# Second expert layer: pairs of token tiles under stationary weights, then single tiles

## The chip, the cores and the metric

One core of a Trainium2 chip runs the whole program. The metric is the device time of one execution in microseconds (us), lower is better. The engines that matter are TensorE (PE in the profile, with its weight loads shown apart as PEld), VectorE (DVE), ScalarE (ACT), GpSimd (POOL) and SyncE (SP), which here only starts transfers. A matmul holds one 128x128 operand still in the array (the stationary operand, brought in by a weight load) and streams the other past it (the moving operand, up to 512 columns).

## The reference

Attention with pooled keys and values makes 4608 tokens of width 512; a dense layer follows, then a routed layer of 8 experts, each token going to one expert:

```python
x = attention(q, k, v)                   # (4608, 512)
h = x @ moe_w_in                         # first layer, width 2048
x = maximum(0.01 * h, h) @ moe_w_out
logits = x @ moe2_w_gate                 # second layer, 8 experts
expert_idx = argmax(logits, axis=1)
for e in range(8):
    m = expert_idx == e
    h = maximum(x[m] @ w1[e], 0)         # w1[e]: 512 x 1024
    out[m] = gate_w[m] * (h @ w2[e])     # w2[e]: 1024 x 512
```

With the reference's inputs the experts get 1165, 549, 12, 0, 597, 0, 571 and 1714 tokens. In tiles of 128 tokens that is 10, 5, 1, 0, 5, 0, 5 and 14, in all 40 tiles.

## The kernel before

Every float32 product is made from two halves, a high part and the rest (index 0 and 1 of an operand), in three passes: high by high, high by rest, rest by high.

*First layer.* The tokens go through in 18 blocks of 256, each in 16 slots, one for each 128 columns of the hidden width. `g1` (L488) multiplies stationary weights with the block's 256 columns in 12 matmuls of 256; ACT and DVE make the activation and its two halves (`ghl`, two buffers); `g2` (L514) uses those halves as stationary operand and streams the weights, 6 matmuls of 512, into the two PSUM banks y0 and y1. `g2` runs two slots behind `g1`. At the end of a block `y_evac` (L529) copies both banks out on ACT. A table of hooks places the attention of later blocks, the splitting of the experts' weights, the logits and the routing in these slots. `step_consts` (L731, in slot 36) prepares constants for the later list of steps.

*Early list.* In the last block, whose slots are counted from k0, `early_1` (slot k0+7) picks the expert with most tokens so far and fetches the list of its first four tiles; `early_2` (slot k0+10) transposes that list on PE (`unpack`, L642) and issues the gathers of its first three tiles. `w_load` brings that expert's weights in four pieces of 2 MB, in slots 9, 10, 11 and 15.

*Second layer.* A step is one tile of 128 tokens of one expert. The token rows are gathered by GpSimd (`m_gather`, L814). `m_xT` (L824) transposes them on PE in four 128x128 transposes, and ACT and DVE write the two halves. `m_g1` (L835) takes the tokens as stationary operand and streams the weights: 2 times 12 matmuls of 512 columns. The hidden rows come out with tokens on the partitions, so `m_hT` (L848) transposes them back on PE, 2 times four transposes, and ACT and DVE write their halves. `m_g2` (L858) does 2 times 12 matmuls of 512; ACT scales the result by the gate (L873) and GpSimd scatters the rows out (L874).

There are two sets of weight tiles (lanes). Steps 0 to 3 use lane 0; later steps alternate. Lane 0 walks the list of tiles from its start, lane 1 from its end. When a lane's expert changes, its next weights are loaded piece by piece behind a condition (`w_next`, L801). The list of the 36 later tiles is made in `final` (L672) and `final_list` (L718), on DVE, once all tokens are routed, while the first two tiles are worked on. Steps 0 to 39 always run, the last three only where the list is that long (L1182).

Of the kernel before, what the change touches and what calls it, by code (L numbers as in the profile page):

```python
# [11 lines left out]
I32 = mybir.dt.int32  # L12
# [9 lines left out]
def kernel(  # L22
# [33 lines left out]
    NX = NSTEP - 3  # L56
    PB = NB - TPB
# [566 lines left out]
    stepc = pool.tile([P, 4], F32, name="stepc")  # L624
# [28 lines left out]
    def early():  # L653
        V = nc.vector
        c = count(0)
        tmp = sb([P, 1, E], F32, "etmp")
        first_max(c, ohs, mb, tmp, 1)
        V.tensor_scalar(out=es, in0=mb, scalar1=-1.0, scalar2=float(E), op0=ALU.mult, op1=ALU.add)
        rows = sb([P, 1], F32, "erow")
        V.scalar_tensor_tensor(  # L660
            out=rows, in0=mb, scalar=-float(CAP), in1=prow, op0=ALU.mult, op1=ALU.add
        )
        ri = sb([P, 1], I32, "eri")
        V.tensor_copy(ri, rows)
        V.tensor_copy(itab[:, NR, 0:1], es)
        V.memset(etab[:, 0:1], -1.0)
        V.tensor_copy(etab[:, 1:2], es)
        V.tensor_scalar(out=rank0, in0=ohs[:, 0], scalar1=4096.0, scalar2=None, op0=ALU.mult)
        V.tensor_tensor(out=rank0, in0=rank0, in1=rev8, op=ALU.add)
        return fetch(ri[0:NE, 0:1], NE, 0)  # L670

    def final(c):  # L672
# [10 lines left out]
        m = sb(sq, F32, "g", 2)  # L683
        key = sb([P, E], F32, "fk")
        V.scalar_tensor_tensor(out=key, in0=n, scalar=float(E), in1=rank0, op0=ALU.mult, op1=ALU.add)
        pre = sb([P, E], F32, "fp")
        end = sb([P, E], F32, "fe")
        ft = sb([P, 4], F32, "ft")
        tot, T, row = ft[:, 0:1], ft[:, 1:2], ft[:, 2:3]
        cv = sb([P, 2], F32, "fcv")  # L690
        V.tensor_reduce(tot, n, axis=AX.X, op=ALU.add)
        V.tensor_tensor(out=m, in0=bc(key, sq, 1), in1=bc(key, sq, 2), op=ALU.is_gt)
        V.tensor_copy(itab[0:1, NR, 1:2], tot[0:1])
        V.tensor_tensor(out=m, in0=m, in1=bc(n, sq, 1), op=ALU.mult)
        V.tensor_reduce(pre, m, axis=AX.X, op=ALU.add)
        V.scalar_tensor_tensor(out=T, in0=stepc[:, 0:1], scalar=tot, in1=stepc[:, 1:2], op0=ALU.mult, op1=ALU.add)
        V.tensor_tensor(out=cv[:, 1:2], in0=stepc[:, 2:3], in1=tot, op=ALU.is_lt)
        V.tensor_tensor(out=end, in0=pre, in1=n, op=ALU.add)
# [5 lines left out]
        V.scalar_tensor_tensor(out=base, in0=iota8, scalar=float(CAP), in1=pre, op0=ALU.mult, op1=ALU.subtract)  # L704
        V.tensor_tensor(out=sel, in0=sel, in1=s2, op=ALU.mult)
        V.scalar_tensor_tensor(out=base, in0=ohs[:, 0], scalar=float(NE), in1=base, op0=ALU.mult, op1=ALU.add)
        V.tensor_tensor(out=s2, in0=sel, in1=iota8, op=ALU.mult)
        V.tensor_tensor(out=base, in0=sel, in1=base, op=ALU.mult)
        V.tensor_reduce(cv[:, 0:1], s2, axis=AX.X, op=ALU.add)
        V.tensor_reduce(row, base, axis=AX.X, op=ALU.add)  # L710
        V.tensor_scalar(
            out=T, in0=T, scalar1=float(E * CAP), scalar2=cv[:, 1:2], op0=ALU.subtract, op1=ALU.mult
        )
        ri = sb([P, 1], I32, "fri")
        V.scalar_tensor_tensor(out=ri, in0=row, scalar=float(E * CAP), in1=T, op0=ALU.add, op1=ALU.add)
        return ri, cv

    def final_list(cv):  # L718
        V = nc.vector
        p = pt("att")  # L720
        for j in range(2):
            nc.tensor.matmul(
                p[0:1, j * 64:j * 64 + NR], cv[0:NR, j:j + 1], ident[0:NR, 0:NR], start=True, stop=True
            )
        er, ch = etab[0:1], sb([1, NR], F32, "fch")
        V.tensor_copy(er[:, 2:], p[0:1, 0:NR])
        V.tensor_copy(itab[0:1, 0:NR, 0], p[0:1, 0:NR])
        V.tensor_tensor(out=ch, in0=er[:, 2:], in1=er[:, 0:NR], op=ALU.not_equal)
        V.tensor_tensor(out=itab[0:1, 0:NR, 1], in0=ch, in1=p[0:1, 64:64 + NR], op=ALU.mult)

    def step_consts():  # L731
        V = nc.vector
        pi = sb([P, 2], I32, "spi")
        pf = sb([P, 2], F32, "spf")
        t, od = pf[:, 0:1], pf[:, 1:2]
        nc.gpsimd.iota(pi[:, 0:1], pattern=[[0, 1]], base=0, channel_multiplier=1)
        V.tensor_copy(stepc[:, 2:3], pi[:, 0:1])
        V.tensor_scalar(out=pi[:, 1:2], in0=pi[:, 0:1], scalar1=1, scalar2=None, op0=ALU.bitwise_and)
        V.tensor_scalar(out=pi[:, 0:1], in0=pi[:, 0:1], scalar1=1, scalar2=None, op0=ALU.arith_shift_right)
# [39 lines left out]
    def hT_view(t, j):  # L779
        return hT_a[:, j] if t % 2 == 0 else vm[j]  # L780

    def lane(t):
        return 0 if t < NE or (t - NE) % 2 else 1
# [12 lines left out]
    def w_regs(s):  # L796
        e = nc.sync.value_load(itab[0:1, s, 0:1], min_val=0, max_val=E - 1)
        c = nc.sync.value_load(itab[0:1, s, 1:2], min_val=0, max_val=1) if s < NR else None
        regs[s] = (e, c)

    def w_next(t, pieces):  # L801
        s2 = t + 2 - NE
        if t < NE - 1 or s2 >= NR:
            return
        if t == NE - 1:
            s2 = 1
        if pieces[0] == 0:
            w_regs(s2)
        e, c = regs[s2]
        w_load(lane(t), pieces, e, c)  # L810
# [3 lines left out]
    def m_gather(t):  # L814
        x = sb([P, DM], F32, "ps", 3)
        n = PB * BLK if t < NE else NT
        nc.gpsimd.indirect_dma_start(
            out=x, out_offset=None, in_=y_d[0:n],
            in_offset=bass.IndirectOffsetOnAxis(ap=gidx[:, t:t + 1], axis=0), bounds_check=n - 1,
            oob_is_err=False,  # L820
        )
        xg[t] = x

    def m_xT(t):  # L824
# [6 lines left out]
        sub(nc.vector, xT2[:, t % 2, :, 1], pv, f32(xT2[:, t % 2, :, 0]))  # L831

# [25 lines left out]
    def m_g2(t, j):  # L858
# [12 lines left out]
        if j == 1:  # L871
            o = sb([P, DM], F32, "kv", 2)
            nc.scalar.activation(o, o_ps.pop(t), AF.Copy, scale=gate[:, t:t + 1])  # L873
            nc.gpsimd.indirect_dma_start(  # L874
                out=out, out_offset=bass.IndirectOffsetOnAxis(ap=sidx[:, t:t + 1], axis=0), in_=o,
                in_offset=None, bounds_check=NT - 1, oob_is_err=False,
            )
# [87 lines left out]
    def early_2():  # L965
        unpack(early_list.pop(0), NE, 0)
        for t in range(3):
            m_gather(t)
# [20 lines left out]
    with tc.manual_schedule():  # L989
# [93 lines left out]
        for s, (b, f) in enumerate(seq):  # L1083
# [31 lines left out]
            if s == k0 + 10:  # L1115
                early_2()
# [3 lines left out]
        m_xT(0)  # L1120
        m_gather(3)
# [5 lines left out]
        m_g1(0, 0)  # L1127
        y_tr(b, 0)
        y_tr(b, 1)
        m_g1(0, 1)  # L1130
        y_logit(b)
        m_hT(0, 0)
        route_a(b)
        m_xT(1)
        m_g2(0, 0)
        m_hT(0, 1)
        route_b(b)
        route_c(b, 0)
        route_c(b, 1)
        m_g2(0, 1)  # L1140
        cnt = count(1)
        m_g1(1, 0)
        ri, cv = final(cnt)
        m_g1(1, 1)
        final_list(cv)
        m_hT(1, 0)
        m_xT(2)
        w_regs(0)
        early_list[0] = fetch(ri[0:NR, 0:1], NR, NE)
        w_load(1, [0, 1], *regs[0])  # L1150
        m_hT(1, 1)

        def steps(t0, t1):
            for t in range(t0, t1):
                m_g1(t, 0)
                if t > t0 or t == 2:
                    m_g2(t - 1, 0)
                m_g1(t, 1)
                w_next(t, [0, 1])
# [3 lines left out]
                if t == 2:  # L1163
                    unpack(early_list.pop(0), NR, NE)
                    m_gather(4)
                    nc.sync.value_load(gidx[0:1, NE:NE + 1], min_val=0, max_val=NT - 1)
                    w_load(1, [2, 3], *regs[0])
                if t > t0 or t == 2:
                    m_g2(t - 1, 1)
                    if t - 1 >= NE - 1:  # L1170
                        w_next(t - 1, [2, 3])
# [5 lines left out]
            if t1 < NSTEP:  # L1177
                w_next(t1 - 1, [2, 3])

        steps(2, NX)  # L1180
# [40 lines left out]
```

## Time and profile before

| | |
|---|---|
| median of 3 runs | 1572.53 us (1563.01 to 1573.03) |
| profiled execution | 1560.74 us |
| its span, first to last instruction | 1559.0 us |
| granted TensorE clock, mean | 0.985 |
| PE busy | 1482.3 us, 95% of the span |
| DVE, ACT, POOL busy | 920.3, 643.8, 327.6 us |

The time of a run is that of the device; the span leaves out what lies before the first and after the last instruction, here 1.7 us. The profiled execution is faster than the fastest of the three others. Busy shares are means over stages that have different limits, so the stretches are read one by one.

### The profile page before, as it was taken

Reading aid. Unit: us, or ns where it says so; the run is one execution under the profiler, and the core shown is the slowest. Engines: PE = TensorE matmul, PEld = TensorE weight load, DVE = VectorE, ACT = ScalarE, POOL = GpSimd, SP = SyncE. Lnnn points to the kernel's source line nnn. Section 1 sums busy time; section 2 is a strip of 40 time slices with the busy share of each in tenths; the row PEclk is TensorE's granted clock in tenths of the full one; section 3 lists DMA queues with packets and bytes.
Section 4 is the critical chain, followed back from the end, with each engine's and each line's share of the span. In section 5 each row is a group of like instructions: output and inputs, shape, how many; then the busy total and the mean of one; then the engine's idle time right before and its main releaser. Section 6 shows DMA issues by size and latency. Waiting matters only on the chain. (4 is left out here: it accounts for less than half of the span.)

```text
span 1559.0 us, 25084 instructions
## 1 busy us (share of the span) xinstructions
PE 1482.3 (95%) x8824; PEld 1296.9 (83%) x8824; DVE 920.3 (59%) x2371; ACT 643.8 (41%) x1442; POOL 327.6 (21%) x294
## 2 busy tenths in 40 slices
PE   4598999999999999999999999999999999999998
PEld 3476889899898898899999899977888888888886
DVE  6998768878878878877878887743111111111111
ACT  4676534544544454544444444322222222222222
POOL 4000012223232222222232233021111111111111
PEclk8799999999999999999999999999999999999999
DMA  9543135456445555545655454064721331661250
GB/s 213 148 134 100 73 127 166 158 198 186 159 150 195 171 183 159 186 154 178 176 167 189 140 181 153 17 238 168 299 84 41 149 147 41 248 264 47 67 231 22
DMA packets 121384, 238.01 MB, mean 153 GB/s; under 512 B 56845, under 2 KB 65041, under 8 KB 117544
## 3 DMA queue, kind: packets, MB, share of 16 engines
q1 hardware_dynamic: 90312, 139.81, 29.0%
q10 hardware_dynamic: 23328, 76.56, 12.9%
q0 software_dynamic: 7616, 20.01, 3.9%
q8 instruction: 71, 1.16, 0.3%
q14 instruction: 57, 0.47, 0.1%
HBM read 418.44 MB, written 87.38 MB: 324 GB/s over the span
## 5 line engine op out<-in xcount | busy, mean ns | idle before, releaser
L522 PE MATMUL y<-w,ghl 128*128 128x512 f32 x1728 | 461.2, 403 | 3.8 <-DVE ghl L128 3.7
L522 PEld LDWEIGHTS y<-w,ghl 128*128 128x128 f32 x1728 | 306.1, 189 | 62.0 <-DVE ghl L128 7.8
L128 POOL TENSOR_TENSOR ps<-ps 128x512 f32<-128x512 f32 x128 | 182.5, 1426 | 477.2 <-ACT ps L125 366.7
L494 PEld LDWEIGHTS h<-x_t,w 128*128 128x128 f32 x1776 | 238.2, 194 | 39.8 <-DVE w L128 18.2
L494 PE MATMUL h<-x_t,w 128*128 128x256 f32 x1776 | 245.7, 288 | 24.0 <-DVE w L128 16.8
L494 PEld LDWEIGHTS y<-x_t,w 128*128 128x128 f32 x1488 | 193.2, 189 | 9.7
L542 DVE CUSTOM_DVE_ANT_0 junk<-y,wg 128x512 bf16<-128x512 f32 x256 | 198.4, 775 | 1.9
L494 PE MATMUL y<-x_t,w 128*128 128x256 f32 x1488 | 196.0, 282 | 0.0
L128 DVE TENSOR_TENSOR at_t<-a,at_t 128x512 fp32r<-128x512 f32 x76 | 52.4, 689 | 203.3 <-ACT at_t L125 203.0
L128 DVE TENSOR_TENSOR vm<-a,vm 128x512 fp32r<-128x512 f32 x40 | 27.7, 692 | 199.3 <-ACT vm L125 199.3
L125 ACT ACTIVATE g<-h 128x256 f32<-128x256 f32 x164 | 62.8, 383 | 146.3 <-PE h L494 134.6
L866 PE MATMUL y<-w,at_t 128*128 128x512 f32 x480 | 120.9, 400 | 1.4 <-ACT at_t L125 0.9
L874 POOL DMA_INDIRECT out_dram<-kv,sidx x40 | 40.4, 1009 | 381.7 <-ACT vm L125 192.0
L866 PE MATMUL y<-w,vm 128*128 128x512 f32 x480 | 120.1, 399 | 0.0
L840 PE MATMUL h<-w,x_t 128*128 128x512 f32 x480 | 118.0, 394 | 0.0
L840 PE MATMUL y<-w,x_t 128*128 128x512 f32 x480 | 118.0, 395 | 0.0
L866 PEld LDWEIGHTS y<-w,at_t 128*128 128x128 f32 x480 | 88.8, 188 | 21.8 <-ACT at_t L125 1.2
L866 PEld LDWEIGHTS y<-w,vm 128*128 128x128 f32 x480 | 88.8, 188 | 19.8
L840 PEld LDWEIGHTS h<-w,x_t 128*128 128x128 f32 x480 | 88.6, 188 | 18.7 <-DVE x_t L128 0.4
L840 PEld LDWEIGHTS y<-w,x_t 128*128 128x128 f32 x480 | 88.6, 188 | 18.2
L502 DVE TENSOR_TENSOR h<-g,h 128x256 f32<-128x256 f32 x132 | 56.0, 424 | 77.9 <-ACT g L125 77.4
L125 ACT ACTIVATE ps<-ps 128x512 fp32r<-128x512 f32 x128 | 80.5, 629 | 21.6 <-DMA ps<-in_moe_w_dram 12.9
(254 smaller groups left out, 1900.8 us busy)
## 6 DMA issues: line engine op xcount, KB each, us to landing
w<-wsp SPq DMA_DIRECT2D x156, 2048.0 KB
wsp<-ps ACTq DMA_DIRECT2D x128, 512.0 KB
ps<-in_moe_w_dram SPq DMA_DIRECT2D x128, 256.0 KB
y_d<-y ACTq DMA_DIRECT2D x18, 512.0 KB
q<-in_q_dram SPq DMA_DIRECT2D x28, 256.0 KB
kv<-in_k_dram SPq DMA_DIRECT2D x24, 288.0 KB
kv<-in_v_dram SPq DMA_DIRECT2D x24, 256.0 KB
ps<-in_moe_w_in_dram SPq DMA_DIRECT2D x8, 512.0 KB
```

Source lines behind the costliest of these rows:

```text
L125: nc.scalar.activation(o, i, AF.Copy, scale=scale)
L128: eng.tensor_tensor(out=o, in0=a, in1=b, op=ALU.subtract)
L494: nc.tensor.matmul(p[:, 0:BLK], win(f)[:, kk, l], xv[:, kk, r], start=(n == 0), stop=(n == 3 * KD - 1))
L502: nc.vector.tensor_tensor(out=g, in0=t, in1=h, op=ALU.max)
L522: nc.tensor.matmul(y_ps[b, i], hl[:, l, i * P:i * P + P], wout(f)[:, r], start=(f == 0 and l + r == 0), stop=(last and l == 1),)
L542: nc.vector.tensor_tensor_reduce(out=jk, in0=y_sb[b][:, i], in1=wg_t[0][:, e], scale=1.0, scalar=0.0, op0=ALU.mult, op1=ALU.add, accum_out ...
L840: nc.tensor.matmul(p, xT2[:, t % 2, kk, l], wlane(lane(t), fh * KD + kk)[:, r], start=(n == 0), stop=(n == 3 * KD - 1))
L866: nc.tensor.matmul(p, d[:, kk, l], wlane(lane(t), 2 * KD + 4 * j + kk)[:, r], start=(j == 0 and n == 0), stop=(j == 1 and n == 11),)
L874: nc.gpsimd.indirect_dma_start(out=out, out_offset=bass.IndirectOffsetOnAxis(ap=sidx[:, t:t + 1], axis=0), in_=o, in_offset=None, bounds_c ...
```

## The change

The second layer's first 28 tiles are worked on as 14 pairs, 2 of the early expert and 12 (`NPS`) of the final list; 12 single tiles follow in the old way, and the three conditional steps.

- A pair has 256 tokens and is treated as a block of the first layer is: `p_g1` holds 128 columns of the weights still and streams the pair's 256 tokens (12 matmuls of 256 columns), `p_h` writes the activation's two halves, `p_g2` uses these as stationary operand (6 matmuls of 512). There are 8 slots for each pair. `m_hT` is not called for pairs. `p_xT` transposes each tile of the next pair in slots 4 and 6, into `x_v` or `atv` in turn.
- Gathers are issued a pair ahead (`p_gather` in slot 1, for the pair after the next), two tiles into one buffer; the results of a pair lie in one buffer of the kind `kv`, scattered by two transfers.
- Each lane takes six pairs of the list in its order: lane 0 the first six, lane 1 the last six. The singles (what is left of each expert) have their lanes from a written list. For the counts above, lane 0 has five pairs of expert 7 and one of expert 0, lane 1 four of expert 0 and two of expert 1; the 12 singles are one tile of expert 1, five of expert 4, five of expert 6 and one of expert 2, in the order 1, 4, 4, 4, 6, 4, 6, 4, 6, 6, 6, 2.
- `step_consts` grows from 10 DVE instructions to 29, `final` from 24 to 36, `final_list` from 4 to some 14. The logits, the routing of the last block and the making of the list move into the slots of the first two pairs.
- `early_2` moves from slot k0+10 to k0+12 and issues four gathers; the fetched lists use the buffer `pn`, not `kv`.

```diff
+    NPS = 12
+    NEP = NE // 2
+    FT = NE + 2 * NPS
+    NSS = NPS + NSTEP - FT
...
     def fetch(rows, n, c0):
-        L = sb([NR, P, 2], F32, "kv", 2)
+        L = sb([NR, P, 2], F32, "pn")
...
+    lanes = [i % 2 for i in range(NPS)] + [1, 0, 0, 0, 1, 0, 1, 0, 1, 1, 1, 0, 1, 0, 1][:NSS - NPS]
...
+    def p_gather(p):
+        x = sb([P, 2, DM], F32, "ps", 3)
+        for i in range(2):
+            m_gather(2 * p + i, x[:, i])
...
+    def xp(p):
+        return atv if p % 2 else x_v
+
+    def p_xT(p, i):
+        x = xg.pop(2 * p + i)
+        d = xp(p)[:, :, :, i * P:i * P + P]
+        b = pt("att")
+        for kk in range(KD):
+            nc.tensor.transpose(b[:, kk * P:kk * P + P], x[:, kk * P:kk * P + P], ident)
+        pv = b.rearrange("p (a n) -> p a n", a=KD)
+        act_copy(d[:, :, 0], pv)
+        sub(nc.vector, d[:, :, 1], pv, f32(d[:, :, 0]))
...
+    def p_g1(p, f):
+        b = pt("h")[:, 0:BLK]
+        n = 0
+        for kk in range(KD):
+            w = wlane(p_lane(p), (f // 4) * KD + kk)[:, :, (f % 4) * P:(f % 4) * P + P]
+            for l, r in ((0, 0), (0, 1), (1, 0)):
+                nc.tensor.matmul(b, w[:, l], xp(p)[:, kk, r], start=(n == 0), stop=(n == 3 * KD - 1))
+                n += 1
+        if f % 4 == 3:
+            w_next(p - NEP, [f // 4])
+        return b
+
+    def p_h(p, f, b):
+        hl = sb([P, 2, BLK], F32R, "ghl", 2)
+        nc.scalar.activation(hl[:, 0], b, AF.Relu)
+        nc.vector.scalar_tensor_tensor(
+            out=hl[:, 1], in0=b, scalar=0.0, in1=f32(hl[:, 0]), op0=ALU.max, op1=ALU.subtract
+        )
+        g_hl[p, f] = hl
+
+    def p_g2(p, f):
+        hl = g_hl.pop((p, f))
+        if f == 0:
+            for i in range(2):
+                o_ps[2 * p + i] = bank(f"y{i}")
+        w = wlane(p_lane(p), 2 * KD + f)
+        for i, l, r in ((0, 0, 0), (0, 0, 1), (1, 0, 0), (1, 0, 1), (0, 1, 0), (1, 1, 0)):
+            nc.tensor.matmul(
+                o_ps[2 * p + i], hl[:, l, i * P:i * P + P], w[:, r], start=(f == 0 and l + r == 0),
+                stop=(f == 7 and l == 1),
+            )
+        if f % 4 == 3:
+            w_next(p - NEP, [2 + f // 4])
+        if f == 7:
+            o = sb([P, 2, DM], F32, "kv", 2)
+            for i in range(2):
+                m_out(2 * p + i, o[:, i])
...
     def early_2():
         unpack(early_list.pop(0), NE, 0)
-        for t in range(3):
-            m_gather(t)
+        for p in range(NEP):
+            p_gather(p)
...
-            if s == k0 + 10:
+            if s == k0 + 12:
                 early_2()
...
-        m_xT(0)
-        m_gather(3)
+        p_xT(0, 0)
+        p_xT(0, 1)
         while pend:
             g2(*pend.pop(0))
...
+        at(0, y_tr, b, 0)
+        at(1, y_tr, b, 1)
+        at(2, y_logit, b)
+        at(2, route_a, b)
+        at(4, route_b, b)
+        at(4, route_c, b, 0)
+        at(4, route_c, b, 1)
+        at(3, p_xT, 1, 0)
+        at(5, p_xT, 1, 1)
+        at(5, final_1)
+        at(6, final_2)
+        at(8, final_3)
+        at(10, final_4)
+        at(14, p_xT, 2, 0)
+        at(15, p_xT, 2, 1)
+        for p in range(NEP, NEP + NPS):
+            if p + 2 < NEP + NPS:
+                at(8 * p + 1, p_gather, p + 2)
+            if p + 1 < NEP + NPS:
+                for i in range(2):
+                    at(8 * p + 4 + 2 * i, p_xT, p + 1, i)
...
+        pend2 = []
+        for p in range(NEP + NPS):
+            for f in range(8):
+                h = p_g1(p, f)
+                run_slot(8 * p + f)
+                pend2.append((p, f))
+                while len(pend2) > (1 if f == 0 or p and f == 7 else 2):
+                    p_g2(*pend2.pop(0))
+                p_h(p, f, h)
...
-        steps(2, NX)
+        def rest():
+            while pend2:
+                p_g2(*pend2.pop(0))
+
+        steps(FT, NX, rest)
```

`final_1` counts and makes the list, `final_2` fetches it, `final_3` writes the experts of the steps and starts lane 1's first weights, `final_4` unpacks the list and gathers pairs 2 and 3. `steps` runs the singles as before, and flushes the last pair's `p_g2` after the first single's first half of `m_g1`.

## Rows read from the trace of the kernel before

**Rows 1.** The page of the profile: busy time, share and instructions of each engine.

```profile
PE 1482.3 (95%) x8824; PEld 1296.9 (83%) x8824; DVE 920.3 (59%) x2371; ACT 643.8 (41%) x1442; POOL 327.6 (21%) x294
```

**Rows 2.** Windows: PE, PEld, DVE, ACT, POOL busy (instructions), granted clock, DMA share, GB/s.

```profile
1020.00:1040.00 20.00, 16.72 (x99) 14.78 (x99) 8.40 (x36) 4.24 (x12) 5.06 (x5) 0.91 0.91 343
...
1160.00:1180.00 20.00, 20.00 (x97) 16.44 (x97) 3.96 (x6) 6.03 (x11) 4.09 (x4) 1.00 0.14 44
```

**Rows 3.** Timeline of PE, one tile of the second layer: start, length, instructions, wait.

```profile
1407.06 0.60 PE L852 MATMUL a<-ident,pr 128*128 128x128 f32 x4
1407.49 0.60 PE L828 MATMUL a<-ident,ps 128*128 128x128 f32 x4
1407.85 3.04 PE L866 MATMUL y<-w,vm 128*128 128x512 f32 x12
1410.73 0.60 PE L852 MATMUL a<-ident,pn 128*128 128x128 f32 x4
...
1419.46 0.60 PE L852 MATMUL a<-ident,pr 128*128 128x128 f32 x4
```

**Rows 4.** Timeline of PE, first layer, from one block into the next.

```profile
996.97 1.55 PE L522 MATMUL y<-w,ghl 128*128 128x512 f32 x6
998.36 3.04 PE L494 MATMUL y<-x_t,w 128*128 128x256 f32 x24
1001.24 1.55 PE L522 MATMUL y<-w,ghl 128*128 128x512 f32 x6
1002.62 1.59 PE L494 MATMUL h<-x_t,w 128*128 128x256 f32 x12
1004.05 1.55 PE L522 MATMUL y<-w,ghl 128*128 128x512 f32 x6
```

**Rows 5.** Groups by shape, from 1000 us on: busy us, mean ns, idle before.

```profile
L873 ACT ACTIVATE kv<-y,gate 128x512 f32<-128x512 f32 x40 | 27.5, 688 | 87.3 <-PE y L866 78.7 <-issue 4.9 <-PE a L629 3.6
...
L494 PEld LDWEIGHTS h<-x_t,w 128*128 128x128 f32 x84 | 11.4, 199 | 0.4
```

**Rows 6.** Timeline of PE around the early list of the second layer.

```profile
1024.07 1.57 PE L522 MATMUL y<-w,ghl 128*128 128x512 f32 x6
1028.92 0.37 PE L645 MATMUL a<-ident,kv 4*128 4x4 f32 x2 [3.28 <-DMA kv<-lst,eri]
1029.22 2.36 PE L494 MATMUL h<-x_t,w 128*128 128x256 f32 x12
...
1033.68 1.59 PE L494 MATMUL h<-x_t,w 128*128 128x256 f32 x12
...
1046.58 0.60 PE L828 MATMUL a<-ident,ps 128*128 128x128 f32 x4
```

**Rows 7.** Line 817 between 1030 and 1036 us: gathers issued, and their landing.

```profile
L817 POOL DMA_INDIRECT ps<-y_d,gidx x3: 992/998/1055, 1030.4 to 1033.1; - x3
...
DMA to landing us min/median/max: 9.1/9.1/9.1
```

**Rows 8.** Who PE waited for, 1020 to 1090 us: us in total, times, longest.

```profile
PE a L645 <- DVE at_t L128: 1.1, 1, 1.1
...
PE y L866 <- DVE at_t L128: 0.5, 2, 0.2
```

**Rows 9.** Timeline of DVE: the final list's first and last instruction (24 in all).

```profile
1066.40 0.17 DVE L676 TENSOR_SCALAR fni<-cnt 128x8 int32<-128x8 f32 x1
...
1069.65 0.16 DVE L715 SCALAR_TENSOR_TENSOR fri<-ft 128x1 int32<-128x1 f32 x1
```

**Rows 10.** Timeline of DVE around the step constants (10 instructions, L737 to L746).

```profile
212.96 0.15 DVE L737 CAST stepc<-spi 128x1 f32<-128x1 int32 x1
...
214.72 0.15 DVE L746 TENSOR_SCALAR stepc<-stepc 128x1 f32<-128x1 f32 x1
...
217.51 0.41 DVE L128 TENSOR_TENSOR ghl<-h,ghl 128x256 fp32r<-128x256 f32 x1
```

**Rows 11.** Timeline of PE over the same stretch.

```profile
217.99 1.70 PE L494 MATMUL h<-x_t,w 128*128 128x256 f32 x12 [1.53 <-DVE ghl L128]
```

More of the change, by code (lines that the diff above doesn't have):

```diff
@@ new lines, in final_list @@
+        V.tensor_copy(itab[0:1, 0:NSS, 0], er[:, 2:2 + NSS])
+        i = 0
+        while i < NSS:
+            j = i + 1
+            while j < NSS and prev_of(j) - prev_of(i) == j - i:
+                j += 1
+            a = 2 + prev_of(i)
+            V.tensor_tensor(out=ch[:, i:j], in0=er[:, 2 + i:2 + j], in1=er[:, a:a + j - i], op=ALU.not_equal)
+            i = j
+        V.tensor_copy(itab[0:1, 0:NPS, 1], ch[:, 0:NPS])
+        V.tensor_tensor(
+            out=itab[0:1, NPS:NSS, 1], in0=ch[:, NPS:], in1=p[0:1, 64 + 2 * NPS:64 + NR], op=ALU.mult
+        )
@@ L779, in hT_view, with prev_of, step_of @@
     def hT_view(t, j):
-        return hT_a[:, j] if t % 2 == 0 else vm[j]
+        return hT_a[:, j] if t % 2 else vm[j]
+    lanes = [i % 2 for i in range(NPS)] + [1, 0, 0, 0, 1, 0, 1, 0, 1, 1, 1, 0, 1, 0, 1][:NSS - NPS]
+    def prev_of(i):
+        same = [x for x in range(i) if lanes[x] == lanes[i]]
+        return same[-1] if same else lanes[i] - 2
+    def step_of(t):
+        return NPS + t - FT
     def lane(t):
-        return 0 if t < NE or (t - NE) % 2 else 1
+        return lanes[step_of(t)]
     def w_load(ln, pieces, e, cond):
@@ L797, in w_regs, with w_next, m_gather @@
         e = nc.sync.value_load(itab[0:1, s, 0:1], min_val=0, max_val=E - 1)
-        c = nc.sync.value_load(itab[0:1, s, 1:2], min_val=0, max_val=1) if s < NR else None
+        c = nc.sync.value_load(itab[0:1, s, 1:2], min_val=0, max_val=1) if s < NSS else None
         regs[s] = (e, c)
-    def w_next(t, pieces):
-        s2 = t + 2 - NE
-        if t < NE - 1 or s2 >= NR:
+    def w_next(i, pieces):
+        ln = lanes[i] if i >= 0 else 0
+        later = [x for x in range(i + 1, NSS) if lanes[x] == ln]
+        if not later or i < -1:
             return
[L805 to L810, printed above, removed]
-    xg, hs, o_ps = {}, {}, {}
-    def m_gather(t):
-        x = sb([P, DM], F32, "ps", 3)
+        if later[0] not in regs:
+            w_regs(later[0])
+        e, c = regs[later[0]]
+        w_load(ln, pieces, e, c)
+    xg, hs, o_ps = {}, {}, {}
+    def p_gather(p):
+        x = sb([P, 2, DM], F32, "ps", 3)
+        for i in range(2):
+            m_gather(2 * p + i, x[:, i])
+    def m_gather(t, x=None):
+        if x is None:
+            x = sb([P, DM], F32, "ps", 3)
         n = PB * BLK if t < NE else NT
@@ L871, in m_g2, with m_out @@
         if j == 1:
+            m_out(t)
+    def m_out(t, o=None):
+        if o is None:
             o = sb([P, DM], F32, "kv", 2)
[L873 to L877, printed above, removed]
+        nc.scalar.activation(o, o_ps.pop(t), AF.Copy, scale=gate[:, t:t + 1])
+        nc.gpsimd.indirect_dma_start(
+            out=out, out_offset=bass.IndirectOffsetOnAxis(ap=sidx[:, t:t + 1], axis=0), in_=o,
+            in_offset=None, bounds_check=NT - 1, oob_is_err=False,
+        )
     seq = []
@@ L1126 @@
         y_evac(b)
[L1127 to L1149, printed above, removed]
@@ L1150, with final_1, final_2, final_3 @@
-        w_load(1, [0, 1], *regs[0])
-        m_hT(1, 1)
-        def steps(t0, t1):
+        hooks.clear()
+        fin = {}
+        def final_1():
+            fin["ri"], fin["cv"] = final(count(1))
+        def final_2():
+            early_list[0] = fetch(fin["ri"][0:NR, 0:1], NR, NE)
+        def final_3():
+            final_list(fin["cv"])
+            w_regs(1)
+            w_load(1, [0, 1], *regs[1])
+        def final_4():
+            unpack(early_list.pop(0), NR, NE)
+            p_gather(NEP)
+            p_gather(NEP + 1)
+            nc.sync.value_load(gidx[0:1, NE:NE + 1], min_val=0, max_val=NT - 1)
+            w_load(1, [2, 3], *regs[1])
@@ L1154, in steps @@
+        pend2 = []
[7 more added lines that the diff above has]
+                p_h(p, f, h)
+        def steps(t0, t1, flush=None):
             for t in range(t0, t1):
                 m_g1(t, 0)
-                if t > t0 or t == 2:
+                if flush:
+                    flush()
+                    flush = None
+                if t > t0:
```

123 lines of the change are left out of this document (75 added, 48 removed).

## Prediction

> **What bounds the kernel now.** I read the busy times first, then stretches of the second layer, then the timeline of PE in the stretches that the change touches. PE is busy 95% of the span and no other engine over 59% [rows 1]. In the steady second layer PE is busy 20.00 of 20 us at a granted clock of 1.00, that is the 2.4 GHz level, with DVE at 3.96, ACT at 6.03 and the transfers at 0.14 [rows 2]. So a step costs what PE needs for it, and whatever is taken off DVE, ACT or GpSimd there is worth nothing by itself. The timeline of PE gives that step: from 1407.06 to 1419.46 us, 12.40 us a tile [rows 3]. It holds four groups of 12 matmuls of 512 columns and three groups of four transposes. Only at the join of the two layers is PE not full: 16.72 of 20 us at clock 0.91 [rows 2]. The reader should see two places: 40 steps that PE alone sets, and some 60 us at the join where other things set the pace.
>
> **A pair against two tiles.** The change keeps the number of streamed columns: a tile's 24 matmuls of 512 in the first product become, for a pair, 96 of 256 (24,576 columns either way), and the second product stays at 48 of 512 a pair. It removes `m_hT`: two transpose groups a tile, four a pair. The price of each form is in the trace, because the first layer already runs the pair's pattern: 12 matmuls of 256 take 1.43 to 1.44 us (two lots from 998.36 to 1001.24), 6 of 512 take 1.38 to 1.39 [rows 4]. I use 1.44 and 1.38.
>
> - Old: 12 matmuls of 512 are two lots of 1.385, 2.77 us; four groups are 11.08; what is left of 12.40 is 1.32, so 0.44 for each transpose group with what it does to its neighbours (they show 0.43 and 0.36 [rows 3]). Two tiles: 24.80 us.
> - New: 8 slots of 1.44 + 1.38 are 22.56, two transpose groups 0.88: 23.44 us.
> - Gain 1.36 us a pair: 1.76 for four transpose groups, less 0.40 because 256 columns at a time cost slightly more than 512. For 14 pairs: 19.0 us.
>
> The 12 singles keep 12.40 us each. The matching work on ACT and DVE falls too, and counts for nothing.
>
> The point on which this stands is that twice as many weight loads in the first product cost only 0.40 us a pair. A load is busy for 199 ns [rows 5], but the 256-column matmul with its own load comes every 120 ns (1.44 / 12) and the 512-column one every 231 (1.385 / 6): 256 columns more cost 111 ns, so some 9 ns a matmul do not scale with columns. The load is hidden. Bounds for an extra load: 0 and 199 ns; I take what the first layer shows, since stationary operand, tile kind and column count are the same there. The Trainium skill says otherwise on its page "TensorE: Matmul & The Clock Gate" (The mechanism): a weight load overlaps matmuls in flight only when it targets another row group, and ours always fill all rows. On the same page (LDWEIGHTS) a load of 128 columns is put at 128 / 1.2 ns; by that rule my estimate is 107 ns more for each of 48 extra loads a pair, 72 us over 14 pairs, and the change would lose. This trace disagrees: 120 ns for 256 columns leaves no room for a load in series.
>
> **The early list.** Before, PE reaches `unpack` at the end of slot k0+10 (1024.07 + 1.57 us) and waits 3.28 us for the fetched list; the next slot, after the pause, takes 4.46 us (1029.22 to 1033.68) instead of 2.82, with the clock down [rows 6]. Two slots later PE comes there at 1025.64 + 2 x 2.82 = 1031.3, and the list has been there since 1028.9. So 3.28 + 1.64 = 4.9 us go away. What is late next is the gathers: they start 1.5 us after `unpack`, about 1.35 apart, and land 9.1 us after issue while the expert's weights come in [rows 6, 7]: tile 0 at 1041.9, tile 1 at 1043.2. PE wants them at 1046.58 - 4.92 = 1041.7 and 1042.1, and the pair's first product needs both. Cost 1.3 us with the copies behind it; 0 if the weights have landed by then, 3 if the weights' last piece, which now starts earlier too, slows them.
>
> **Waits at the join.** Before, beside the early list, PE loses 3.1 us there in four kinds of wait (the first and the last shown [rows 8]), on `m_hT` copies and on DVE behind the list. These go with the order of work. New ones:
>
> - `final` grows from 24 to 36 DVE instructions. It took 3.41 us (1066.40 to 1069.81 [rows 9]), 0.142 each, so 5.1 now. `p_h` of slot 5 queues behind it on DVE, after the copy of `p_xT`: ready some 7.4 us after the hook. PE has 2.82 + 2.82 until `p_g2` of that slot plus four matmuls on the high half, 0.92: 6.6. Wait 0.8 (0 to 3).
> - `final_4` in slot 10 gathers pair 2 while lane 1 loads 8 MB. Issue some 3.3 us into that slot, landing 9.1 later [rows 7], wanted 12.7 us into it (slot 14 after its `p_g1`): 0.3 (0 to 3). `final_2` and `final_3` wait for nothing that is not due: three slots, 8.5 us, lie between the list and its first reader on PE. Of SP only the loads queue behind the read of the list, and lane 1 is wanted in slot 24.
> - The first single has no older `m_g2` between the transposes of the next tile and its `m_g1`. A Relu, two ACT copies and a DVE copy, at some 0.65 us each (the nearest row has 0.69 [rows 5]) with hand-overs, take 2.75 after the second `m_g1`; PE has three transpose groups, 1.3, to fill it. Wait 1.5 us (0 to 2.5).
>
> Sum of new ones 3.9 us (0 to 11.5), against 3.1 gone. The logits, routing and transposes of the last block are moved, not added.
>
> **Pair boundaries.** Both result banks are evacuated at once, 0.69 us each on ACT [rows 5], with the next pair's Relu queued behind. PE has two lots of 12 matmuls, 2.88 us, before it writes a bank again. Need: 1.38 for the copies, some 0.4 each for the Relu and the rest (256 columns on DVE took 0.41 [rows 10]) and 0.2 for hand-overs, 2.4. The first layer's block end is the same pattern and runs without a wait (1001.24 follows 998.36 by just two lots [rows 4]). Cost 0; 0.5 us slack covers it; at 1 us a copy it would be 0.1 a pair.
>
> **Step constants.** 19 more DVE instructions in slot 36. The ten take 1.92 us (212.96 to 214.88) and PE then waits 1.53 us for the `ghl` copy behind them on DVE [rows 10, 11]. No cover there: the wait grows by the whole addition, 19 x 0.142 = 2.7 to 19 x 0.192 = 3.6. I take 3.0.
>
> **Weights.** Before, the lanes change experts six times after the first load; by the written orders after it is six too (lane 1: 0, 1, 6; lane 0: 0, 4, 2). Each 8 MB has at least a whole pair of the other lane, 23 us, and mostly 37. Cost 0.
>
> **Sum.** 19.0 + 4.9 + 3.1 - 3.9 - 3.0 = 20.1 us. Against its own execution: 1560.74 - 20.1 = 1540.6. That execution is 11.8 us below the median of the three runs, two of which lie near 1573 and one at 1563; the difference is not in the stretches that are changed, so I take the 20.1 from the median: 1552.4, say 1552 us.
>
> **Rivals.**
> - *The gain is eaten at the join.* All new waits at their upper ends, 11.5 in place of 3.9, and 3.6 for the constants: gain 11.9, 1560.6 us, within 1%. For it: the early list shows that one wait there costs more than its length, because the clock drops with it. Against it: before, the other waits left the clock at its upper level.
> - *Weight loads in series*, the slower side. Place: every `p_g1`. Price: up to 0.199 us [rows 5] for 672 extra loads, 134 us, some 1686; it turns the change into a loss from 20.1 / 672 = 30 ns a load. For it: PEld is busy 83% [rows 1] and the lanes are written by transfers while they are read. Against it: rows 4, taken in a layer that has such transfers as well. The Trainium skill's page "TensorE: Matmul & The Clock Gate" (The mechanism), cited above, would give this rival.
> - *The pairs don't fill.* The list could need more steps than before. With the tile counts, half of each expert's remaining tiles gives 5 + 5 + 2 + 2 + 2 = 16 pairs, 12 are taken, and 12 singles remain, 40 in all: no change in steps. If it failed, 1572.
>
> **How the numbers follow.** Forecast 0.66, eaten at the join 0.24, loads in series 0.07, not filled 0.03. About 1% is what a measurement of this kernel can tell from no change, 15.7 us; the forecast is past it, the second and fourth rivals aren't. So faster 0.66, same 0.27, slower 0.07. Range: the best case of the sum (no new wait, constants at 2.7) is a gain of 24.3, off the lowest of the runs (1563.01) about 1538; the join's worst with a few us of unseen waits is a gain of some 6 off the median, 1566. Loads in series lie outside.
>
> **What would show it.** After: `p_g1` lots 1.44 us apart and slots of 2.82; pairs 23.4 us long at a full PE; no wait on the fetched list; a longer `ghl` wait near 218 us; waits on gathers, on `p_h` in slot 7 and at the first single of 1 us or so. Slots over 2.9 us in steady pairs, or a clock below 1.00 at the join, would make the prediction wrong.

## The result, and the profile after

| | before | after |
|---|---|---|
| median (range, runs) | 1570.28 us (1563.01 to 1574.33, 8) | 1556.05 us (1551.87 to 1561.14, 8) |
| profiled execution, its span | 1560.74, 1559.0 us | 1558.05, 1556.0 us |
| mean granted clock | 0.985 | 0.975 |

The ratio is 0.9914 [0.9887, 0.9941]: 0.86% faster, some 14 us, where 20.1 were forecast. By the interval the change is faster, but the gain is under the 15.7 us (1%) that the prediction took as its line between faster and same. The two profiled executions differ by 2.7 us only, so the profiles are compared by stretches that lie close together, and totals by the medians.

The page's busy line after, for [rows 1]:

```profile
PE 1472.8 (95%) x9272; PEld 1317.6 (85%) x9272; DVE 939.4 (60%) x2468; ACT 626.8 (40%) x1442; POOL 327.3 (21%) x294
```

PE is again the bound. It runs 448 instructions more in less time: 1344 matmuls of 256 columns in place of 672 of 512, and 224 transposes fewer. The windows, for [rows 2] (the first two lie at the join, which now ends later; columns as there):

```profile
1080.00:1100.00 20.00, 19.28 (x123) 17.18 (x124) 5.26 (x28) 3.85 (x9) 4.24 (x5) 1.00 0.71 277
1100.00:1120.00 20.00, 11.24 (x61) 9.86 (x60) 2.56 (x5) 1.97 (x4) 2.83 (x3) 0.74 0.54 225
1160.00:1180.00 20.00, 20.00 (x131) 18.17 (x130) 4.35 (x9) 4.70 (x11) 4.09 (x4) 1.00 0.16 53
```

The steady pairs are full at the upper level, as the steady tiles were. The hole is at 1100 to 1120 us: PE busy 11.24 of 20 at clock 0.74, a stretch in which the prediction expected 0.3 us of wait and the full clock. The chain of PE's waits from 1000 us on (total, times, longest):

```profile
PE a L900 <- DMA ps<-y_d,gidx: 9.1, 2, 8.8
PE a L965 <- DVE vm L132: 1.0, 1, 1.0
PE y L935 <- DVE ghl L923: 0.9, 1, 0.9
```

One wait is 8.8 us long, on gathered token rows. The timeline of PE there, of the first steps of the final list:

```profile
1099.28 1.59 PE L914 MATMUL y<-at_t,w 128*128 128x256 f32 x12
1109.63 1.09 PE L900 MATMUL a<-ident,ps 128*128 128x128 f32 x4 [8.76 <-DMA ps<-y_d,gidx]
1110.37 2.91 PE L935 MATMUL y<-w,ghl 128*128 128x512 f32 x6
1113.08 1.91 PE L914 MATMUL h<-at_t,w 128*128 128x256 f32 x12
1114.83 0.60 PE L900 MATMUL a<-ident,ps 128*128 128x128 f32 x4
```

and windows of 4 us over the same stretch (columns as above):

```profile
1096.00:1100.00 4.00, 4.00 (x28) 3.64 (x27) 0.53 (x2) 0.77 (x2) 2.21 (x3) 1.00 0.98 412
...
1104.00:1108.00 4.00, 0.00 (x0) 0.00 (x0) 0.00 (x0) 0.00 (x0) 0.00 (x0) 0.50 1.00 424
1108.00:1112.00 4.00, 2.37 (x8) 2.11 (x9) 0.61 (x1) 0.60 (x1) 0.00 (x0) 0.50 0.69 275
1112.00:1116.00 4.00, 4.00 (x23) 3.57 (x23) 0.50 (x2) 0.92 (x2) 0.00 (x0) 0.78 0.00 1
1116.00:1120.00 4.00, 4.00 (x25) 3.50 (x24) 1.12 (x2) 0.45 (x2) 0.00 (x0) 1.00 0.01 2
```

PE waits 8.76 us for the rows of pair 2. During the pause the granted clock falls to 0.50, the 1.2 GHz level, and it is back at 1.00 after 1116. So what follows the pause, from 1109.63 to 1114.83, takes 5.2 us; four transposes (0.44 by the prediction's working), 6 of 512 and 12 of 256 are 3.3 at full clock. The hole costs some 10.7 us. Who issued those gathers late is in GpSimd's timeline:

```profile
1087.14 1.02 POOL L991 DMA_INDIRECT out_dram<-kv,sidx  x1 [4.83 <-ACT kv L990]
1097.18 0.98 POOL L991 DMA_INDIRECT out_dram<-kv,sidx  x1 [9.02 <-ACT ghl L922]
1098.46 1.05 POOL L876 DMA_INDIRECT ps<-y_d,gidx  x1 [0.30 <-issue]
...
1102.44 1.00 POOL L876 DMA_INDIRECT ps<-y_d,gidx  x1 [0.30 <-issue]
```

The first pair's two scatters (L991) stand ahead of the gathers (L876) in GpSimd's order, while lane 1's first 8 MB load (DMA share 0.98 and 1.00 in the windows above). The second scatter waits 9.02 us and is issued 10.04 behind the first; the four gathers, whose list PE has unpacked at 1088.93, queue behind it. The wait is written into the program: it is a semaphore instruction in GpSimd's own stream, here in the view of L991 from 1060 to 1130 us (shortest, median and longest in ns):

```profile
L991 POOLq EVENT_SEMAPHORE  x5: 17/1637/9351, 1081.1 to 1126.9; - x5
```

The timeline names ACT as what ended it, but ACT's copies for both tiles were done at 1087.20. What it waits for is the landing of the first scatter; a later run names that. Of landings this trace has the second scatter's, 8.6 us after issue, and the last gather's, 10.2; PE goes on 11.2 us after the issue of the first gather (1098.46 to 1109.63).

From the store of the last first-layer block to the end, before has 509.5 us (1049.5 to 1559.0) and after 498.6 (1057.4 to 1556.0): the second layer gains 10.9 with that hole in it. The steady pair is in PE's timeline (12 x 256 is `p_g1`, 6 x 512 is `p_g2`, L900 the transposes of the next pair's tiles; x24 and x12 are two lots in a row):

```profile
1165.07 1.60 PE L914 MATMUL h<-x_t,w 128*128 128x256 f32 x12
1166.51 1.56 PE L935 MATMUL y<-w,ghl 128*128 128x512 f32 x6
1167.90 3.04 PE L914 MATMUL y<-x_t,w 128*128 128x256 f32 x24
1170.77 1.56 PE L935 MATMUL y<-w,ghl 128*128 128x512 f32 x6
...
1176.43 0.60 PE L900 MATMUL a<-ident,ps 128*128 128x128 f32 x4
...
1182.52 0.60 PE L900 MATMUL a<-ident,ps 128*128 128x128 f32 x4
...
1188.57 1.60 PE L914 MATMUL h<-at_t,w 128*128 128x256 f32 x12
```

From 1165.07 to 1188.57: 23.50 us, against 2 x 12.40 [rows 3]. A pair begins inside the x24 at 1167.90, and the next lot follows at 1170.77 with no wait: the boundary is free.

The early list, for [rows 6], on PE:

```profile
1043.16 0.39 PE L649 MATMUL a<-ident,pn 4*128 4x4 f32 x2
...
1053.49 0.60 PE L900 MATMUL a<-ident,ps 128*128 128x128 f32 x4
1054.40 0.66 PE L900 MATMUL a<-ident,ps 128*128 128x128 f32 x4 [0.31 <-DMA ps<-y_d,gidx]
```

No wait on the list; the pair's second tile waits 0.31 us for its gather, and 0.91 lie between the two transposes. The step constants, for [rows 11], on PE and on DVE (first and last of 29 instructions):

```profile
221.05 2.93 PE L498 MATMUL h<-x_t,w 128*128 128x256 f32 x12 [3.95 <-DVE ghl L132]
223.78 1.06 PE L410 MATMUL a<-ident,pn 128*128 128x128 f32 x4
```

```profile
213.60 0.15 DVE L768 CAST spf<-spi 128x1 f32<-128x1 int32 x1
...
217.79 0.15 DVE L765 TENSOR_SCALAR stepc<-stepc 128x1 f32<-128x1 f32 x1
```

DVE takes 4.34 us (213.60 to 217.94) where ten took 1.92 [rows 10], and PE waits 3.95 us where it waited 1.53. Again the clock falls with the pause: the 12 matmuls behind it take 2.73 us (221.05 to 223.78) instead of 1.44. The stores of the blocks stand 0.65 us later than before ahead of this step and 5.45 behind it: 4.8 us in all.

In the profiled execution the rest of the first layer, whose code is unchanged, puts on another 6.3 us up to the last block, and the longest wait of PE there for `at_t`, a tile of the attention that DVE finishes, is 2.2 us instead of 0.9. That is the second question for the experiments.

### The profile page after: what moved, and what is told of

It is laid out like the page before. It is cut to its first block, busy times and chain, and to the rows that moved or that the text cites. A ratio compares the mean times of both kernels' runs of the same rounds, so it can differ in the third digit from the quotient of the medians.

```text
span 1556.0 us, 25769 instructions
## 1 busy us (share of the span) xinstructions
PE 1472.8 (95%) x9272; PEld 1317.6 (85%) x9272; DVE 939.4 (60%) x2468; ACT 626.8 (40%) x1442; POOL 327.3 (21%) x294
## 5 line engine op out<-in xcount | busy, mean ns | idle before, releaser
L526 PE MATMUL y<-w,ghl 128*128 128x512 f32 x1728 | 466.3, 406 | 2.8 <-DVE ghl L132 2.5
L526 PEld LDWEIGHTS y<-w,ghl 128*128 128x128 f32 x1728 | 310.1, 192 | 61.7 <-DVE ghl L132 6.3
L935 PE MATMUL y<-w,ghl 128*128 128x512 f32 x672 | 176.5, 401 | 0.9 <-DVE ghl L923 0.9
L935 PEld LDWEIGHTS y<-w,ghl 128*128 128x128 f32 x672 | 120.4, 190 | 22.4 <-DVE ghl L923 1.3
L991 POOL DMA_INDIRECT out_dram<-kv,sidx x40 | 40.1, 1003 | 382.5 <-ACT kv L990 199.3
L923 DVE SCALAR_TENSOR_TENSOR ghl<-h,ghl 128x256 fp32r<-128x256 f32 x56 | 23.8, 425 | 135.9 <-ACT ghl L922 135.9
L132 DVE TENSOR_TENSOR at_t<-a,at_t 128x512 fp32r<-128x512 f32 x62 | 42.7, 688 | 87.6 <-ACT at_t L129 87.2
L129 ACT ACTIVATE ghl<-h 128x256 fp32r<-128x256 f32 x132 | 50.7, 384 | 92.9 <-PE y L526 42.8
L129 ACT ACTIVATE ghl<-y 128x256 fp32r<-128x256 f32 x124 | 47.3, 382 | 95.2 <-DVE y L506 50.5
L132 DVE TENSOR_TENSOR x_t<-a,x_t 128x512 fp32r<-128x512 f32 x60 | 41.1, 688 | 51.7 <-ACT x_t L129 51.7
L129 ACT ACTIVATE g<-y 128x256 f32<-128x256 f32 x124 | 47.4, 382 | 60.9 <-PE y L498 53.4
L295 DVE TENSOR_TENSOR kv<-kv 72x512 f32<-72x512 f32 (+8 forms) x126 | 68.0, 540 | 3.2
L613 POOL DMA_INDIRECT lst<-ent,six x36 | 37.8, 1051 | 150.4 <-DVE six L612 115.1
```

Source lines behind the costliest of these rows:

```text
L129: nc.scalar.activation(o, i, AF.Copy, scale=scale)
L132: eng.tensor_tensor(out=o, in0=a, in1=b, op=ALU.subtract)
L295: eng.tensor_tensor(out=o, in0=t[:, :, 0:w], in1=t[:, :, w:2 * w], op=ALU.add)
L526: nc.tensor.matmul(y_ps[b, i], hl[:, l, i * P:i * P + P], wout(f)[:, r], start=(f == 0 and l + r == 0), stop=(last and l == 1),)
L613: nc.gpsimd.indirect_dma_start(out=lst, out_offset=bass.IndirectOffsetOnAxis(ap=ix[:, 0:1], axis=0), in_=ent[:, i, :], in_offset=None, bou ...
L923: nc.vector.scalar_tensor_tensor(out=hl[:, 1], in0=b, scalar=0.0, in1=f32(hl[:, 0]), op0=ALU.max, op1=ALU.subtract)
```

## The experiments

The ratio is always to the kernel before, run beside it on the same chip.

**Do the scatters or the load hold the gathers?** Two cures, each taking one suspect away from the changed kernel.

```diff
-                m_out(2 * p + i, o[:, i])
+                m_out(2 * p + i, o[:, i], late_out if p == 0 else None)   # scatter kept back
         at(10, final_4)
+        at(11, flush_out)                                               # scatters issued here
```

> The changed kernel, with the two scatters of the first pair issued on GpSimd after the gathers of pairs 2 and 3 instead of before them; its loads, lists and all else are the same. Theory (order on GpSimd's queue: the pair's second scatter waits for the first to land, 8.6 us under lane 1's load, and the gathers stand behind it): the first gather starts 1.5 us after the list is unpacked instead of 9.2, PE's wait for it falls from 8.8 us to 0 to 1.5, no fall of the clock there, the time is 9 to 11 us below the changed kernel. Rival (bandwidth alone: the gathers land when the 8 MB of lane 1 are through, whatever the order): the wait stays over 6 us, the time within 3 us of the changed kernel's.

Measured 1549.91 us, ratio 0.9882 [0.9854, 0.9911]. GpSimd's timeline:

```profile
1084.65 1.01 POOL L640 DMA_INDIRECT pn<-lst,fri  x1 [4.47 <-DVE ghl L923]
1093.95 1.03 POOL L876 DMA_INDIRECT ps<-y_d,gidx  x1 [8.29 <-issue]
...
1097.90 1.00 POOL L876 DMA_INDIRECT ps<-y_d,gidx  x1 [0.30 <-issue]
1099.21 1.02 POOL L1003 DMA_INDIRECT out_dram<-kv,sidx  x1 [0.30 <-issue]
```

The gathers start 9.3 us after the list's fetch (1084.65, the GpSimd instruction ahead of them) instead of 17.2 (1081.30 to 1098.46). They still take 9.2 to 16.3 us to land under the load, and yet PE has no wait at pair 2. The order on GpSimd was what made them late, and not the load alone.

```diff
-            w_load(1, [0, 1], *regs[1])          # final_3, slot 8
-            w_load(1, [2, 3], *regs[1])          # final_4, slot 10
+        at(16, final_5)                          # all four pieces
```

> The changed kernel, with lane 1's first 8 MB started in slot 16 instead of slots 8 and 10; the order on GpSimd stays as changed. Both theories expect PE's wait for the gathers to go. By the order on the queue the second scatter still stands ahead of the gathers, but waits about 3 us for the first instead of 9.0, and the gathers land in about 4 us: the time 9 to 11 us below the changed kernel. Lane 1 is wanted in slot 24, some 22 us after the load starts; a wait of up to 3 us there would show that this cure has its own price.

Measured 1548.47 us, ratio 0.9876 [0.9846, 0.9906]; GpSimd's timeline:

```profile
1086.39 1.02 POOL L991 DMA_INDIRECT out_dram<-kv,sidx  x1 [4.83 <-ACT kv L990]
1090.05 0.98 POOL L991 DMA_INDIRECT out_dram<-kv,sidx  x1 [2.63 <-DVE gate L655]
1091.33 1.05 POOL L876 DMA_INDIRECT ps<-y_d,gidx  x1 [0.30 <-issue]
```

In the same order without the load, scatters land in 2.7 to 2.8 us and gathers in 3.5 to 4.6. The second scatter follows 3.66 us behind the first, and no wait is left at pair 2, nor in slot 24 where lane 1 is wanted. So the hole needs both: the order and the load. From the last block's store to the end both take 488 us (488.1, 487.8): 10.5 and 10.8 less than the change. By the ratios the two are 5 to 8 us better than the change, less than the 9 to 11 expected.

**The early list alone, from both sides.** First the changed kernel with the list where before had it:

```diff
-            if s == k0 + 12:
+            if s == k0 + 10:
```

> The changed kernel, with the early list unpacked in slot k0+10 again instead of k0+12. By the prediction's step the wait of 3.3 us for the list comes back with a slot slowed by the clock (1.6 us), and the waits for the first gathers go (0.7 us): 4 us above the changed kernel. Rival (the wait only changes its place, since the gathers would then be what PE waits for): no more than 1 us of difference.

Measured 1562.61 us, ratio 0.9952 [0.9928, 0.9977], against 0.9914 with the list late. The timeline of PE shows the wait again, and the slow slot behind it (5.29 us up to 1051.52):

```profile
1045.93 0.37 PE L649 MATMUL a<-ident,pn 4*128 4x4 f32 x2 [3.62 <-DMA pn<-lst,eri]
1046.23 2.93 PE L498 MATMUL h<-x_t,w 128*128 128x256 f32 x12
...
1051.52 1.64 PE L498 MATMUL h<-x_t,w 128*128 128x256 f32 x12
```

Then the opposite edit in the kernel before, and nothing else of the change:

```diff
-            if s == k0 + 10:
+            if s == k0 + 12:
```

> The kernel before with one edit of the change alone: early_2 two slots later, as the change has it; single tiles throughout. My account: the wait of 3.28 us for the early list and the long slot behind it go, the first gathers wait up to 1 to 3 us in their place, so 2 to 5 us below the kernel before (ratio 0.997 to 0.9987), and the last block of the first layer is 3 to 4 us shorter in the profile. Rival: the wait only moves to the gathers, no change.

Measured 1566.52 us, ratio 0.9959 [0.9938, 0.9981], -6.4 us. No wait on the list; the first gathers cost 1.56 us instead:

```profile
1046.06 0.40 PE L645 MATMUL a<-ident,kv 4*128 4x4 f32 x2
...
1058.12 0.63 PE L828 MATMUL a<-ident,ps 128*128 128x128 f32 x4 [1.56 <-DMA ps<-y_d,gidx]
```

So the early list gains by itself, 6.4 us net of the gathers where 3.6 were forecast, with an interval of 3.0 to 9.7.

**The step constants, from both sides.** Moved to slot 29 in the changed kernel:

```diff
-        at(36, step_consts)
+        at(29, step_consts)
```

> The changed kernel, with the step constants' 29 DVE instructions in slot 29, where DVE is idle more than half the time, instead of slot 36. If they stand in PE's way in slot 36 as predicted, PE's wait for the activation there falls from 4.0 us to 0.5 or less and the slots after it run at the full clock: the time 4 to 6 us below the changed kernel. Rival (the stall moves with them or comes back at the next DVE-bound slot): within 1.5 us.

Measured 1558.37 us, ratio 0.9932 [0.9905, 0.9959]: no gain by this number. In the profile PE's wait in slot 36 falls from 3.95 us to 0.30, and that block is 6.0 us shorter (45.2 to 39.1 between the stores of blocks 1 and 2); but later, at 300 to 312 and 408 to 420 us, the clock fell in this execution and took it back. Alone it was inconclusive, and the expected 4 to 6 us were missed. So the kernel before got the added work instead, 19 small dependent DVE instructions whose result nothing uses:

```diff
+        d = sb([P, 1], F32, "rmx", 2)
+        V.tensor_copy(d, stepc[:, 3:4])
+        for _ in range(18):
+            V.tensor_scalar(out=d, in0=d, scalar1=1.0, scalar2=None, op0=ALU.subtract)
```

> The kernel before with 19 more small dependent VectorE instructions on a scratch tile in slot 36, whose results nothing uses. My account: the wait in that slot grows from 1.5 us to about 4, the granted clock falls behind it, and the kernel is 4 to 5 us slower (ratio about 1.003). Second question: if the longer waits later in the first layer come from this step, they show here too (longest of the waits for at_t 2.2 us instead of 0.9). Rival: TensorE's other work hides it, 0 to 1 us.

Measured 1577.97 us, ratio 1.0038 [1.0018, 1.0058], +6.0 us. PE's timeline:

```profile
221.15 2.93 PE L494 MATMUL h<-x_t,w 128*128 128x256 f32 x12 [4.98 <-DVE ghl L128]
223.87 1.05 PE L406 MATMUL a<-ident,pn 128*128 128x128 f32 x4
```

The wait is 4.98 us and the block 6.2 us longer (40.4 to 46.6). The longest of the waits for `at_t` stays 0.8 us, so the longer ones do not come from this step.

**Both kernels once more,** to see what an execution of the same code varies by.

> The kernel before, once more, for a second profile. In the first layer, from 230 to 1000 us, the first profile of before shows no fall of the granted clock, those of the changed kernel and of the four experiments one to four, each after a wait of PE of 1 to 2 us, and each profile loses 2 to 6 us there. Theory (the falls come and go from run to run in either kernel): this profile shows one or more and is some 5 us longer than the first one. Rival (the change brings them): none here.

> The changed kernel, once more, on the chip of the three others, as their measure. The wait for the gathers of pair 2 comes again with 8 to 9 us and the clock at its lower level; the time 11 to 16 us below before.

Before: 1567.81 us, ratio 0.9995 [0.9975, 1.0015]; its profile has one fall of the clock in the first layer (at 784 us) and is 1.5 us longer than the first one, where 5 were expected. After: 1558.07, ratio 0.9925 [0.9902, 0.9948]. In the profile of the change the hole is there again (7.4 us of wait, 8 to 9 expected).

**Cures together.** The changed kernel with the constants in slot 29 and one of the two cures, then with both:

> The changed kernel with both cures: the first pair's scatters behind the gathers, and the step constants in slot 29. If the two stalls are independent of each other, their gains add: 9 for the gathers, and 4 to 6 for the constants, 13 to 15 us below the changed kernel. Rival (the first layer gives the constants' gain back, as the run with the constants alone suggests): 7 to 10 us below the changed kernel, with the stall in slot 36 gone and other falls of the clock in the first layer.

> The changed kernel with lane 1's first load in slot 16 and the step constants in slot 29. Same two expectations as for the kernel with the scatters behind the gathers: 13 to 15 us below the changed kernel if the gains add, 7 to 10 if the constants' gain is given back. Against that kernel within 3 us, since either cure frees the gathers.

> The changed kernel with late scatters, a late load and the step constants in slot 29, all three. My account: either cure alone takes the wait of the second pair's gathers away whole, so the two don't add: within 3 us of the runs that had one of them with the constants (1543 to 1544 us, ratio 0.983 to 0.985). Rival: the load and the scatters cost separately, another 5 us or more.

| cures | median | ratio |
|---|---|---|
| late scatters, constants in 29 | 1543.37 us | 0.9838 [0.9812, 0.9863] |
| late load, constants in 29 | 1544.24 us | 0.9835 [0.9812, 0.9858] |
| all three | 1545.86 us | 0.9831 [0.9795, 0.9867] |

Each is 0.9% of the kernel before, some 14 us, better than the change (0.9925, run beside the first two). Scatters and load do not add: they cure one wait. All three beat both kernels by more than any interval. The table also isolates the cures: with the constants in slot 29 alone the ratio was 0.9932, so freeing the gathers is worth some 15 us by the ratios (10.5 and 10.8 by the stretch); with the gathers freed alone it was 0.9882 and 0.9876, so moving the constants is worth 6.9 and 6.4 us. Each of these ratios is uncertain by some 6 us. That the second scatter of a pair waits for the first to land is named in the timeline of GpSimd of the last one. Whether the results would still be right without that wait is not tested.

```profile
1097.35 1.02 POOL L1003 DMA_INDIRECT out_dram<-kv,sidx  x1 [0.30 <-issue]
1102.41 0.99 POOL L1003 DMA_INDIRECT out_dram<-kv,sidx  x1 [4.04 <-DMA out_dram<-kv,sidx]
```

**The unchanged first layer.** The change widens three small tiles, which shifts the buffers behind them. The kernel before with that layout alone, the instructions as they were:

```diff
-stepc = pool.tile([P, 4], F32
+stepc = pool.tile([P, 6], F32
-pi = sb([P, 2], I32, "spi")
+pi = sb([P, 4], I32, "spi")
-pf = sb([P, 2], F32, "spf")
+pf = sb([P, 6], F32, "spf")
```

> The kernel before with the three small tiles as wide as the change has them (stepc 6, spi 4, spf 6 columns), so that the buffers behind them lie where the change puts them; its instructions and their order are those of before. My account: no change, ratio 0.999 to 1.001, longest wait for at_t 0.9 us. Rival: the place of the buffers lengthens the first layer's waits (longest 2.2 us) and costs 3 to 6 us, ratio 1.002 to 1.004.

Measured 1572.17 us, ratio 1.0012 [0.9987, 1.0037]: no effect that shows, though the interval reaches to a cost of 0.4%. Its longest wait for `at_t` was 1.7 us in the profile, between the 0.9 expected and the 2.2 of the rival.

The answer came from the kernel before with the late list, whose first layer is that of before up to the last block. Windows of 4 us, then the timeline of PE:

```profile
304.00:308.00 4.00, 4.00 (x20) 3.71 (x20) 1.86 (x6) 1.74 (x3) 0.00 (x0) 0.56 0.12 50
...
416.00:420.00 4.00, 4.00 (x18) 3.81 (x17) 1.13 (x2) 1.16 (x3) 0.00 (x0) 0.50 0.00 0
```

```profile
657.32 1.60 PE L494 MATMUL h<-x_t,w 128*128 128x256 f32 x12
661.13 0.65 PE L355 MATMUL a<-ident,q 128*128 128x128 f32 x4 [2.21 <-DVE at_t L128]
```

It has the long wait (2.21 us at 661, before 0.9 at most) and the falls of the clock, without the change. From 230 to 1000 us, where all kernels have the same code, the time at the lower level was 0 and 3.4 us in the two profiles of before, 20.5 here, 17.1 with the layout alone, 3.4 with the extra instructions, and 3.4 to 27.3 in the nine profiles of the change and its variants. So it varies by the execution. The two profiles of before, 1560.74 and 1562.22 us, are at the low end of that kernel's runs (1562 to 1584).

From the store of block 2 to that of the last block but one the five profiles with the first layer of before take 742 to 756 us, the nine others 748 to 758. How far each profiled execution lies from its kernel's median can be put on this stretch, as an estimate: then both kinds come to 751 us on average (750 to 752, and 747 to 755). So the 6.3 us are not shown to be the change's own. The long wait is another matter: some 2.2 us at 651 to 661 us stands in all nine profiles of the change's kind and in one of the five others. The change may bring it on; which edit would is not shown. What starts a fall of the clock is not settled.

## Why the prediction was right, and where its terms were off

- **Pairs: right.** 14 x 1.36 = 19.0 was forecast, 14 x (24.80 - 23.50) = 18.2 measured. The loads are hidden: a lot of 12 still takes 1.43 to 1.44 us. The sentence of the Trainium skill ("TensorE: Matmul & The Clock Gate", The mechanism) by which they would run in series is contradicted by this trace too, 120 ns for a matmul of 256 columns with its load. The same section also lets a load into the background weight buffer run ahead of matmuls in flight, which the prediction left out; the 120 ns agree with that, and no run here shows the buffer itself.
- **Early list: right.** 4.9 less 1.3 for the first gathers; the pair of experiments gives -6.4 us [-9.7, -3.0] in the kernel before, and +4 to +6 (0.9952 against 0.9925 and 0.9914, give or take 5 to 6) where it is undone.
- **Gathers of pair 2: the step that failed.** "`final_4` in slot 10 gathers pair 2 ... 0.3 (0 to 3)" was worked out from issue to landing, with an issue 3.3 us into the slot. (By these numbers, 3.3 + 9.1 against 12.7, there were 0.3 us to spare; it was entered as a wait.) The landing was some 1 to 2 us longer than 9.1 (10.5 us for the first gather in the second profile of the change, at most 11.2 in the first one). The issue was far off: two scatters stand ahead on GpSimd and the second waits for the first. From the list's fetch the gathers start after 17.2 us instead of the 9.3 that they take with the scatters behind them; with that and the landing of that run, 9.2, the first would have been there at 1081.3 + 9.3 + 9.2 = 1099.8, before PE came (1100.87). Measured 8.76 and 1.9 of low clock, 10.7 us. The prediction followed SP's queue and left out GpSimd's, though the scatters of a pair were in the diff. A clock below 1.00 at the join was among its own signs of being wrong, and it came.
- **Step constants: mis-sized.** "I take 3.0" was above the wait (+2.42, under its bounds of 2.7 to 3.6), but the clock falls behind it: 4.8 in the profile (3.9 to 4.8 in the five that have the step in slot 36), 6.0 [2.8, 9.1] when put on the kernel before. The prediction named this effect at the join and did not price it here.
- **Other new waits: right.** 0.91 for `p_h` behind the final list (0.8), 1.02 at the first single (1.5), 0.3 on the first gathers (1.3; 0.3 to 2.0 where the list is late, by the execution).
- **Sum.** 18.2 + 4.9 + 3.1 - 0.3 - 0.9 - 10.7 - 1.0 - 4.8 = 8.5 us, where medians show 11.8 to 14.2: some 3 to 6 us are unassigned, of which the second layer's own stretch has 2.2 (10.9 measured, 18.2 + 3.1 - 0.9 - 10.7 - 1.0 = 8.7 worked out). With the hole cured that stretch is 21.4 and 21.7 us shorter than before where 19.4 is worked out, so the 2.2 do not lie in the hole. The rival "eaten at the join" happened in part: one wait there of 10.7 us, of a kind that was priced at 3 at most, in place of many small ones. It did not take all, because the early list and the pairs paid in full. The time lies in the range, but by the prediction's own line of 15.7 us it belongs to "same", which had a chance of 0.27, and not to "faster" with 0.66. That two losses, 10.4 and 1.8 us over their terms, cost the forecast only 6 to 8 us is partly luck: the unassigned gain makes up for some of it.

## What to carry to other kernels

When work is regrouped, follow the order of every engine that issues transfers, and what each of them waits for, with the landing time that holds under the load of that moment: two stores that are in nobody's way when they land in 2.7 us hold up the gathers behind them when they take 8.6. Price a new wait of PE of several microseconds at its length and some 2 us more for the clock that falls with it (1.5 to 2.7 in the places measured here). Compare one execution's stretches around the edit, and look at the unchanged stretches first: they tell how much a single execution is off.

## What was not expected of the hardware

- Two scatters into one tensor, back to back on GpSimd, went one after the other: the second was issued 3.66 us behind the first on quiet transfer engines, 10.04 with a load of weights running. It is the program that waits there (the semaphore instruction above), so this is no property shown of the chip; the landing time that sets the length of the wait is.
- The same kinds of transfers took 2.7 to 2.8 (scatter) and 3.5 to 4.6 us (gather) on quiet engines, 8.6 (scatter) and 9.2 to 16.3 (gather) beside a load that kept them at a share of 1.0.
- The granted clock fell to the 1.2 GHz level at each of these pauses of PE: 3.28, 3.62, 3.95, 4.98 and 8.76 us. In unchanged code it also fell behind pauses of 0.7 and 1.7 us in one execution (302.76 and 413.52 us in the kernel before with the late list), and did not behind 2.21 in the same one or 1.09 in the kernel before (408.45). Why one and not the other stays open.
